# Spreading the second layer's weight conversion, summing its rows on VectorE, and adding the last two halves in the output transposes

## The chip, the core and the metric

One NeuronCore of a Trainium2 chip runs the whole program. The metric is device microseconds (us) of one execution. A profile shows one such execution, engine by engine: PE (TensorE matmuls), PEld (its weight loads), DVE (VectorE), ACT (ScalarE), POOL (GpSimd), SP (SyncE, which issues nearly all DMAs).

## What is computed

```python
# x: (2, 4096, 192), weight: (8, 7); softmax over the 7 taps
x_pad = concatenate([zeros((B, 6, D)), x], axis=1)
out = einsum('hk,bskhg->bshg', softmax(weight), windows_of_7(x_pad))   # depthwise causal convolution
x = out.reshape(8192, 192)

h = x @ w_in1                                   # (8192, 2048)
g = where(h >= 1, h, where(h <= -1, 0, (h + 1) ** 2 / 4))
x = g @ w_out1                                  # (8192, 192)

h = x @ w_in2
g = s * maximum(h, 0) ** 2 + b
return g @ w_out2                               # (8192, 192)
```

All inputs and the output are float32. Because `b` is one number, its part of the result is `b` times the sum of `w_out2` over its 2048 rows: one row of 192 biases that is added to every token.

## The kernel before

Tokens are cut into 16 blocks of 512 and `d_ff` into 16 tiles `f` of 128. A unit is one block and one tile of one layer: the first product (192 deep, giving 128 hidden rows by 512 tokens in one PSUM bank of pool `h`), the nonlinearity on ACT and DVE, and the second product, accumulated over the 16 tiles in two banks of pool `a` (128 and 64 of the 192 columns). Two blocks run side by side, so a **step** `k` is one pair of units, numbered `u = 2k` and `2k + 1`; TensorE takes them as two 64-row halves at once. There are 257 steps. Layers alternate in the order 6, 4, 4, 6, 6, 6 blocks (layer 1, layer 2, layer 1, ...), so layer 2 starts at step 48 (`u = 96`), and its tile `f` is first used at `u = 96 + 2f`.

Every operand is split into a high and a low fp32r part. For a unit of layer 1 ACT computes L1077 and L1084, DVE takes a maximum (L1090), ACT or DVE casts the high part (L385 or L387) and DVE subtracts for the low part (L1112). In layer 2 it is L1098, L1105, the cast and L1112. So each step has two L1112, and counting them tells how far DVE has come.

The weights arrive as raw words and are converted in **pieces** of two tiles (`piece`, L512): three loads on SP into one of two `raw` buffers (L523, L532, L538), then on ACT L562 and two casts, and on DVE nine instructions (L569, L577, L591, L598, L624, twice L635, L645, L654). Eight pieces hold layer 2. Line 1322 on gives piece `i` its due unit:

```python
    u0, u1 = SECOND
    for i, _ in enumerate(PIECES[1]):
        need = u0 + (u1 - u0) * (i + 1) / len(PIECES[1])
```

A block that is not convolved on TensorE is loaded by SP (L689), turned by DVE (L699) and convolved on DVE with one L715 and six L726. The 64 remaining channels of a pair of blocks are spread to both halves of the partitions by two copies SBUF to SBUF on SP's queue (L775) before they are split (L385 or L387, then L791).

The order on every engine is made ahead of time by a planner (`Plan.run`, L122). It gives each operation a priority, mostly its unit plus an offset, and a planned duration, and lets each engine take the best operation that can start. A DMA is planned at 500 ns of SP's time and 2100 ns until it has landed (L389). Engines then run their lists in order; a wait holds up all that stands behind it on the engine.

`emit_bias` (L1157) is called when the first block of layer 2 ends (after step 63). It sums `w_out2` with 16 matmuls against a matrix of ones (L1163), copies and adds the pieces of the sum (L1174, L1183), turns it (L1192) and multiplies it by `b` (L1201). The evacuation of every layer 2 block (`evac_second`, L1212) adds that bias: ACT scales 128 columns (L1225) and one half of the other 64 (L1243), then DVE adds the second half (L1252). The last two blocks leave by `put_rows` (L1293): TensorE turns 128 tokens at a time (L1300, L1301), ACT copies them out of PSUM (L385) and SP issues one DMA for each 128 tokens (L1314).

Of the kernel before, what the change touches and what calls it, by code (L numbers as in the profile page):

```python
# [28 lines left out]
SLOT, DRAIN = 232.0, 400.0  # L29


PIECES = ((1, 1) + (2,) * 7, (2,) * 8)
# [178 lines left out]
def kernel(  # L211
# [12 lines left out]
    nc = tc.nc  # L224
    B, S, D = x.shape
# [4 lines left out]
    NF = DFF // P  # L230
    NT = B * S
    NBLK = NT // NB
# [6 lines left out]
    UP, DN = slice(0, DB), slice(DB, 2 * DB)  # L239
# [6 lines left out]
    pl = Plan()  # L246

    def fixed(name, shape, dt=F32):
        return Buf(ap=const.tile(shape, dt, name=name))
# [31 lines left out]
    ident = fixed("ident", [P, P])  # L281
    ones = fixed("ones", [P, P], F32R)
# [4 lines left out]
    sb2 = fixed("sb2", [P, 2])  # L287
    bias = fixed("bias", [P, 2])
    taps = fixed("taps", [H, KT])
    band = fixed("band", [P, HG * SUB])  # L290
    toep = fixed("toep", [P, H * WIN])
    stat = fixed("stat", [H, 2])
    wsm = {"A": fixed("tapsA", [P, KT]), "B": fixed("tapsB", [P, KT])}

    def heads(_):
# [27 lines left out]
        for e in range(HG):  # L323
# [16 lines left out]
        reads=(half,),  # L340
        writes=(warm,),
# [20 lines left out]
        reads=(ident,),  # L362
        writes=(ones,),
# [546 lines left out]
    def units(k):  # L910
# [206 lines left out]
    def w_out_of(l, f):  # L1117

        i, o = at[l, f]
        return wF[l, i].ap[:, o, :]  # L1120
# [35 lines left out]

    def emit_bias(u):  # L1157

        p, row, col = Buf("h"), Buf("f"), Buf("f")
# [7 lines left out]
        ws = [wF[1, i] for i in range(len(PIECES[1]))]  # L1167
        pl.op(u + 2.6, ("pe", SLOT * NF + DRAIN), sums, reads=(ones, *ws), writes=(p,))

        for c0, c1, o in ((P, D, D), (0, P, ROW - 2 * P)):  # L1170
            pl.op(
                u + 2.7,
                act_ps(D),
                lambda _, c0=c0, c1=c1, o=o: nc.scalar.copy(  # L1174
                    row.ap[:, c0:c1], p.ap[:, o : o + c1 - c0]
                ),
                reads=(p,),
                parts=(row,),
            )
        pl.op(  # L1180
            u + 2.8,
            dve1(D),
            lambda _: nc.vector.tensor_tensor(  # L1183
                row.ap[:, 0:D], row.ap[:, 0:D], p.ap[:, 0:D], op=ALU.add
            ),
            reads=(p,),
            writes=(row,),
        )
        pl.op(
            u + 2.8,  # L1190
            dve1(D),
            lambda _: nc.vector.transpose(out=col.ap[:, 0:D], in_=row.ap[:, 0:D]),  # L1192
            reads=(row,),
            writes=(col,),
        )
        for b in range(0, D + DB, HALO):
            q, c = slice(b % P, b % P + HALO), b if b < D else b - DB
            pl.op(
                u + 2.9,
                ("dve", 120.0),  # L1200
                lambda _, b=b, q=q, c=c: nc.vector.tensor_scalar(  # L1201
                    bias.ap[q, b // P : b // P + 1],
                    col.ap[q, c : c + 1],
                    sb2.ap[q, 1:2],
                    None,
                    op0=ALU.mult,
                ),
                reads=(col, sb2),
                parts=(bias,),
            )  # L1210

    def evac_second(u, j):  # L1212

        pA, pB = acc.pop((1, j))
        q = j % 2
        me, ot = (UP, DN)[:: 1 - 2 * q]
        yA = Buf("f")
        if q == 0:
            stored["y"] = Buf("f")
        yB = stored["y"]  # L1220

        def scale(e):
            to = yA.ap[:, 0:NB]
            if e == "act":
                nc.scalar.activation(  # L1225
                    to, pA.ap, AF.Identity, bias=bias.ap[:, 0:1], scale=sb2.ap[:, 0:1]
                )
            else:
                nc.vector.tensor_scalar(
                    to, pA.ap, sb2.ap[:, 0:1], bias.ap[:, 0:1], op0=ALU.mult, op1=ALU.add  # L1230
                )

        pl.op(
            u + 3,
            (act_ps(NB, 186.0), dve1(NB, 122.0)),
            scale,
            reads=(pA, bias, sb2),
            writes=(yA,),
        )
        got = pl.op(  # L1240
            u + 3,
            act_ps(NB, 186.0),
            lambda _: nc.scalar.activation(  # L1243
                yB.ap[me, 0:NB], pB.ap[ot], AF.Identity, bias=bias.ap[me, 1:2], scale=sb2.ap[me, 0:1]
            ),
            reads=(pB, bias, sb2),
            parts=(yB,),
        )
        got = pl.op(
            u + 3.2,  # L1250
            dve1(NB, 61.0),
            lambda _: nc.vector.scalar_tensor_tensor(  # L1252
                out=yB.ap[me, 0:NB],
                in0=pB.ap[me],
                scalar=sb2.ap[me, 0:1],
                in1=yB.ap[me, 0:NB],
                op0=ALU.mult,
                op1=ALU.add,
            ),
            reads=(pB, sb2),  # L1260
            parts=(yB,),
            after=(got,),
        )
        if j >= NBLK - 2:
            put_rows(u, j, me, yA, yB, got)
            return
        put_blocks(u, yA, ((j, 0, 0, P),))
        if q:
            put_blocks(u, yB, ((j - 1, 0, P, DB), (j, DB, P, DB)))
# [20 lines left out]
                    reads=(t,),  # L1290
                )

    def put_rows(u, j, me, yA, yB, got):  # L1293

        for t in range(TT):
            p, y = Buf("h"), Buf("f")
            c = slice(t * P, (t + 1) * P)
# [5 lines left out]
            pl.op(  # L1303
                u + 5, ("pe", 500.0), turn, reads=(yA, ident), writes=(p,), parts=(yB,), after=(got,)
            )
            pl.op(
                u + 5,
                (act_ps(D), dve1(D)),
                lambda e, p=p, y=y: copy(e, y.ap[:, 0:D], p.ap[:, 0:D]),
                reads=(p,),  # L1310
                writes=(y,),
            )
            to = out[j * NB + t * P : j * NB + (t + 1) * P, :]
            dma(u + 6, lambda _, to=to, y=y: nc.sync.dma_start(out=to, in_=y.ap[:, 0:D]), reads=(y,))  # L1314


    todo = {}
# [3 lines left out]

    u0, u1 = SECOND
    for i, _ in enumerate(PIECES[1]):
# [10 lines left out]
    for i, v in enumerate((s_in, b_in)):  # L1334
        dma(
            2,
            lambda _, i=i, v=v: nc.sync.dma_start(
                out=sb2.ap[:, i : i + 1], in_=v.to_broadcast([P, 1])
            ),
            parts=(sb2,),  # L1340
            after=third,
        )

    for k in range(steps):
        for q in range(2):
            n = k + GATE - LAG * q
            if 0 <= n < len(rows[q]):
                l, j, f = rows[q][n]
# [5 lines left out]
        for q in range(2):  # L1354
# [3 lines left out]
            if l == 0 and f == 0 and j + 2 < NBLK:  # L1358
# [59 lines left out]
```

## Time and profile before

| what | us |
|---|---|
| three runs | 1200.47, 1202.11 (median), 1202.85 |
| the profiled execution | 1200.08 |
| its span, first to last instruction | 1198.1 |
| TensorE busy in the span | 1179.8 (98%) |
| VectorE busy | 808.5 (67%) |
| ScalarE busy | 863.6 (72%) |
| granted TensorE clock, mean share of full speed | 0.993 |

The profiled execution has 2.0 us outside its span, and it is 2.0 us shorter than the median run. The busy share of TensorE counts an overlap of two matmuls once, so it does not tell whether they follow each other at their best pace; the distance between the same place of two steps tells that.

### The profile page before, as it was taken

To read this page: it belongs to the slowest core of one execution; us is meant where nothing else is said; L and a number is where in the kernel's file an instruction comes from. 1 tells how busy PE (TensorE), PEld (TensorE's weight loads), DVE (VectorE), ACT (ScalarE), POOL (GpSimd) and SP (SyncE) were. 2 spreads that over 40 slices of the span, in tenths; PEclk is the share of its full clock that TensorE was granted. 3 is DMA by queue.
4 is the path that set the end of the run, shared out by engine and by line. 5 is a ranking of instruction groups with operands and counts; after the bars stand their busy time and mean duration, and the time that the engine had idled before them with its cause. 6 is when DMAs were issued, how large, how long until landed. Compare 5 with 4: busy or idle time off the path is not lost.

```text
span 1198.1 us, 24944 instructions
## 1 busy us (share of the span) xinstructions
PE 1179.8 (98%) x9900; PEld 1059.2 (88%) x9900; DVE 808.5 (67%) x1373; ACT 863.6 (72%) x1571; POOL 53.8 (4%) x528
## 2 busy tenths in 40 slices
PE   8899999999999999999999999999999999999998
PEld 7778887888889999898889888899899889999997
DVE  5997999995555696975444455787966754455543
ACT  5876878776666777787666676777777776676765
POOL 1000000000000000000000000000000000000000
PEclk8999999999999999999999999999999999999999
DMA  5431033200021111000002021111000000020100
GB/s 139 97 72 52 1 82 71 72 1 19 1 36 25 23 36 30 1 19 1 19 8 38 2 45 29 27 29 20 7 13 10 10 1 19 1 45 1 28 1 27
DMA packets 104171, 34.76 MB, mean 29 GB/s; under 512 B 86653, under 2 KB 100471, under 8 KB 104055
## 3 DMA queue, kind: packets, MB, share of 16 engines
q1 hardware_dynamic: 103703, 32.94, 13.1%
q8 instruction: 77, 1.26, 0.5%
q14 instruction: 39, 0.32, 0.1%
q10 hardware_dynamic: 352, 0.25, 0.1%
HBM read 19.53 MB, written 6.29 MB: 22 GB/s over the span
## 4 chain that ended last, share of the span: by engine, by line
PE 88%; DVE 7%; ACT 2%; DMA 1%; issue 1%; POOL 0%; SPq 0%; DVEq 0%; POOLq 0%; ACTq 0%
PE a L1019 46%; PE h L957 41%; DVE o L1112 1%; DVE f L1090 1%; DVE w L577 1%; DMA f<-x 1%; DMA x<-x 1%; DVE z L598 0%; DVE w L635 0%; PE h L894 0%; ACT f L1077 0%; ACT o L385 0%; DVE w L624 0%; PE h L472 0%; DVE z L591 0%
## 5 line engine op out<-in xcount | busy, mean ns | idle before, releaser
L1019 PE MATMUL a<-o,w 64*128 64x512 f32 (+1 forms) x5080 | 695.1, 393 | 2.6 <-ACT o L385 1.3
L1019 PEld LDWEIGHTS a<-o,w 64*128 64x128 f32 (+1 forms) x5080 | 544.7, 185 | 63.6 <-POOL seen L947 3.9
L957 PE MATMUL h<-o,w 64*128 64x512 f32 x3048 | 457.1, 392 | 2.4 <-POOL seen L947 2.4
L957 PEld LDWEIGHTS h<-o,w 64*128 64x128 f32 x3048 | 329.9, 185 | 35.6 <-POOL seen L947 6.3
L1112 DVE TENSOR_TENSOR o<-f,o 128x512 fp32r<-128x512 f32 x346 | 233.7, 687 | 15.3 <-ACT o L385 9.4
L957 PE MATMUL h<-o,wB 64*128 64x512 f32 x1536 | 234.0, 393 | 5.1 <-DVE f L1090 3.9
L385 ACT CAST o<-f 128x512 fp32r<-128x512 f32 x274 | 167.1, 621 | 42.8 <-DVE f L1090 36.4
L957 PEld LDWEIGHTS h<-o,wB 64*128 64x128 f32 x1536 | 166.1, 185 | 25.2 <-DVE f L1090 6.3
L1098 ACT ACTIVATE f<-h 128x512 f32<-128x512 f32 x167 | 95.0, 595 | 109.6 <-PE h L957 109.2
L387 DVE CAST o<-f 128x512 fp32r<-128x512 f32 x105 | 44.6, 426 | 166.2 <-ACT f L1105 166.0
L1090 DVE TENSOR_TENSOR f<-f,h 128x512 f32<-128x512 f32 x179 | 118.5, 681 | 43.9 <-ACT f L1084 43.5
L1077 ACT ACTIVATE f<-h 128x512 f32<-128x512 f32 x179 | 101.6, 595 | 47.0 <-PE h L957 46.1
L1112 DVE TENSOR_TENSOR o<-x,o 128x512 fp32r<-128x512 f32 x166 | 113.4, 687 | 6.0 <-ACT o L385 3.0
L1084 ACT ACTIVATE f<-f 128x512 f32<-128x512 f32 x179 | 108.5, 633 | 0.5
L1105 ACT ACTIVATE f<-f 128x512 f32<-128x512 f32 x167 | 101.0, 633 | 0.2
L947 POOL MEMSET seen<- 1x1 f32 x506 | 48.8, 96 | 1126.0 <-PE a L1019 566.2
L1098 ACT ACTIVATE x<-h 128x512 f32<-128x512 f32 x89 | 52.2, 595 | 63.5 <-PE h L957 63.4
L385 ACT CAST o<-x 128x512 fp32r<-128x512 f32 x132 | 81.1, 621 | 13.6 <-DVE x L1090 12.1
L387 DVE CAST o<-x 128x512 fp32r<-128x512 f32 x57 | 24.2, 425 | 96.6 <-ACT x L1105 94.7
L1090 DVE TENSOR_TENSOR x<-x,h 128x512 f32<-128x512 f32 x77 | 51.5, 681 | 29.6 <-ACT x L1084 29.4
L1077 ACT ACTIVATE x<-h 128x512 f32<-128x512 f32 x77 | 44.5, 594 | 24.2 <-PE h L957 24.2
L1105 ACT ACTIVATE x<-x 128x512 f32<-128x512 f32 x89 | 55.5, 633 | 0.1
(119 smaller groups left out, 489.6 us busy)
## 6 DMA issues: line engine op xcount, KB each, us to landing
raw<-in_moe_w_out_dram SPq DMA_DIRECT2D x15, 384.0 KB
f<-in_x_dram SPq DMA_DIRECT2D x58, 68.0 KB
raw<-in_moe_w_in_dram SPq DMA_DIRECT2D x15, 256.0 KB
out_dram<-f SPq DMA_DIRECT2D x44, 64.0 KB
out_dram<-x SPq DMA_DIRECT2D x40, 64.0 KB
f<-f SPq DMA_DIRECT2D x20, 128.0 KB
raw<-in_moe_w_in_dram SPq DMA_DIRECT2D x18, 128.0 KB
x<-f SPq DMA_DIRECT2D x16, 128.0 KB
```

Source lines behind the costliest of these rows:

```text
L385: nc.scalar.copy(to, v)
L387: nc.vector.tensor_copy(to, v)
L577: lambda _: nc.vector.scalar_tensor_tensor(out=w(True), in0=words(1), scalar=0x80000000, in1=z(True), op0=ALU.bitwise_and, op1=ALU.bitwise_or,
L947: i = nc.gpsimd.memset(seen.ap, 0.0)
L957: i = nc.tensor.matmul(h.ap, w[r], m.ap[r], start=start and n == 0, stop=stop and n == len(terms[0]) - 1,)
L1019: i = nc.tensor.matmul(p.ap, w()[r], m.ap[r], start=first and start and at_n == 0, stop=last and stop and at_n == 2,)
L1077: lambda _: nc.scalar.activation(R(), h.ap, IDENTITY_SAT15_5, scale=15.5),
L1084: lambda _: nc.scalar.activation(R(), R(), AF.Square, bias=0.5, scale=1.0 / 31.0),
L1090: lambda _: nc.vector.tensor_tensor(R(), R(), h.ap, op=ALU.max),
L1098: lambda _: nc.scalar.activation(R(), h.ap, AF.Relu),
L1105: lambda _: nc.scalar.activation(R(), R(), AF.Square),
L1112: lambda _: nc.vector.tensor_tensor(gl.ap, R(), gh.ap.bitcast(F32), op=ALU.subtract),
```

## The change

1. `SECOND` goes from `(56, 94)` to `(64, 124)`: the due unit of piece `i` of layer 2 was `60.75 + 4.75 i` (the last one at 94) and is now `71.5 + 7.5 i` (the last one at 124, the first use of its tiles).
2. `emit_bias` no longer sums `w_out2` on TensorE. As pieces become ready, 15 additions of 128x512 on DVE add up the tiles, two short ones fold the parts, and one float32 matmul of 192 columns against the ones sums over the partitions. One ACT copy takes the place of two copies and an addition.
3. For the last two blocks, the 64-column bank is scaled as a whole (128 partitions, both halves) by ACT, and a float32 matmul with `twice` (the identity's two halves added, 128x64) adds the two halves while it turns them. DVE's L1252 is gone there. Two groups of 128 tokens share an output tile, so four DMAs of twice the size replace eight.

```diff
-SECOND = (56, 94)
+SECOND = (64, 124)
...
+    twice, bias1 = toep.ap[:, 0 : D - P], toep.ap[:, D - P : D - P + 1]
...
     def emit_bias(u):
...
-        def sums(_):
-            for f in range(NF):
-                nc.tensor.matmul(
-                    p.ap, ones.ap, w_out_of(1, f)[:, P:ROW], start=(f == 0), stop=(f == NF - 1)
-                )
...
+        for f in range(1, NF):
+            pl.op(
+                u - 2 * NF + 2 * f + 4,
+                dve1(N),
+                lambda _, f=f: nc.vector.tensor_tensor(
+                    T(0, N), F(0) if f == 1 else T(0, N), F(f), op=ALU.add
...
+        for c0, c1, o in ((P, D, D), (0, P, N - P)):
...
+                    T(c0, c1), T(c0, c1), T(o, o + c1 - c0), op=ALU.add
...
+            lambda _: nc.tensor.matmul(p.ap[:, 0:D], ones.ap.bitcast(F32), T(0, D)),
...
+            lambda _: nc.scalar.copy(row.ap[:, 0:D], p.ap[:, 0:D]),
...
     def evac_second(u, j):
...
+        if j >= NBLK - 2:
+            yB = Buf("f")
+            pl.op(
+                u + 2.9,
+                ways,
+                lambda e: scale(e, yB, pB, bias1),
+                reads=(pB, toep, sb2),
+                writes=(yB,),
+            )
+            put_rows(u, j, yA, yB)
+            return
...
-                nc.tensor.transpose(p.ap[:, P:D], yB.ap[me, c], ident.ap[me, me])
...
+                nc.tensor.matmul(p.ap[:, P:D], yB.ap[:, c], twice)
...
+                        out=to, in_=y.ap[:, 0 : 2 * D].rearrange("p (t d) -> p t d", t=2)
```

In the lists below a row is a source line, an operation, the tile it writes and those it reads; lines of the changed kernel are its own (a few more than before).

SP's list where layer 2's first pieces are loaded (`moe2`), before the change; `f7<-x2` and `f0<-x2` are the SBUF copies of the first convolved pair, and `raw0`, `raw1` are the two load buffers:

```order
L523 DMA raw1_64<-in_moe2_w_in_dram 128x2x256
L532 DMA raw1_64<-in_moe2_w_in_dram 128x1x256
L538 DMA raw1_64<-in_moe2_w_out_dram 128x2x384
L775 DMA f7_74<-x2_106 64x512 x2
L775 DMA f0_67<-x2_106 64x512 x2
L523 DMA raw0_63<-in_moe2_w_in_dram 128x2x256
```

And the same place in the changed kernel, where the rows ahead of it are the load of the first piece alone:

```order
L540 DMA raw1_64<-in_moe2_w_out_dram 128x2x384
L777 DMA f7_74<-x2_106 64x512 x2
L777 DMA f3_70<-x2_106 64x512 x2
L525 DMA raw0_63<-in_moe2_w_in_dram 128x2x256
L534 DMA raw0_63<-in_moe2_w_in_dram 128x1x256
```

Three pieces stood ahead of those copies, the third one directly; now one does, and the second piece's load stands behind them. In the same way the next copies (from `x1`) stood directly behind the eighth piece's load; they now stand behind the fifth one's.

DVE's list in step 44 before the change, with a whole piece (`w1_7`) between the additions of two steps:

```order
L577 SCALAR_TENSOR_TENSOR w0_66<-raw0_63,z0_65 128x768
L791 TENSOR_TENSOR o14_92<-x0_104,o16_94 128x512
L591 TENSOR_SCALAR z0_65<-w0_66 128x768
L759 TENSOR_TENSOR o21_99<-f8_75,o17_95 128x512
L598 SCALAR_TENSOR_TENSOR z0_65<-raw0_63,z0_65 128x768
L1090 TENSOR_TENSOR f10_77<-f10_77,h3_110 128x512
L624 TENSOR_TENSOR w0_66<-w0_66,w1_7_152 128x640
L1090 TENSOR_TENSOR x2_106<-x2_106,h0_107 128x512
L635 TENSOR_TENSOR w1_7_152<-w0_66,z0_65 128x2x256
L635 TENSOR_TENSOR w1_7_152<-w0_66,z0_65 128x2x64
L1112 TENSOR_TENSOR o6_84<-f10_77,o7_85 128x512
```

The same steps of the changed kernel (`x0` holds the running sum of L1172, and `w1_5` is the sixth piece):

```order
L593 TENSOR_SCALAR z0_65<-w0_66 128x768
L1092 TENSOR_TENSOR x2_106<-x2_106,h3_110 128x512
L1092 TENSOR_TENSOR f8_75<-f8_75,h0_107 128x512
L600 SCALAR_TENSOR_TENSOR z0_65<-raw0_63,z0_65 128x768
L1114 TENSOR_TENSOR o5_83<-x2_106,o24_102 128x512
L1114 TENSOR_TENSOR o14_92<-f8_75,o18_96 128x512
L626 TENSOR_TENSOR w0_66<-w0_66,w1_5_150 128x640
L1172 TENSOR_TENSOR x0_104<-x0_104,w1_4_149 128x512
L1092 TENSOR_TENSOR x2_106<-x2_106,h2_109 128x512
L1092 TENSOR_TENSOR f4_71<-f4_71,h1_108 128x512
L637 TENSOR_TENSOR w1_5_150<-w0_66,z0_65 128x2x256
L1114 TENSOR_TENSOR o22_100<-x2_106,o1_79 128x512
```

The eighth piece was done by step 45; now the sixth is under way there, and the eighth is done in step 53. The additions of the bias sum stand between.

PE's list where the bias is summed, before the change (`a` are accumulators of layer 2, `h_107` the bank of the sum):

```order
L1019 MATMUL a_114<-o_103,w_7_152 128x512
L1019 MATMUL a_112<-o_79,w_7_152 128x512
L1163 MATMUL h_107<-w_0_145,ones 128x512 x2
...
L1163 MATMUL h_107<-w_7_152,ones 128x512 x2
L1019 MATMUL a_112<-o_93,w_7_152 128x512
```

And in the changed kernel:

```order
L1021 MATMUL a_113<-o_98,w_7_152 128x512
L1021 MATMUL a_112<-o_86,w_7_152 128x512
L1191 MATMUL h_107<-x_104,ones 128x192
L1021 MATMUL a_112<-o_90,w_7_152 128x512
L1021 MATMUL a_113<-o_96,w_7_152 128x512
```

Sixteen matmuls of 512 columns became one of 192, at the same place.

## Rows read from the trace of the kernel before

**Rows 1.** The page: engines' busy time, and the chain that ended last, by engine.
```profile
PE 1179.8 (98%) x9900; PEld 1059.2 (88%) x9900; DVE 808.5 (67%) x1373; ACT 863.6 (72%) x1571; POOL 53.8 (4%) x528
...
PE 88%; DVE 7%; ACT 2%; DMA 1%; issue 1%; POOL 0%; SPq 0%; DVEq 0%; POOLq 0%; ACTq 0%
```

**Rows 2.** The chain in order of time (start, length, what), two like places of steps.
```profile
1131.03 1.40 PE h L957 x12
...
1175.15 1.40 PE h L957 x12
```

**Rows 3.** L1112 alone in one stretch: length, busy (count), PEclk, DMA share, GB/s.
```profile
118.85:300.55 181.70, 52.10 (x79) 0.99 0.17 41
```

**Rows 4.** The same stretch in four: PE, PEld, DVE, ACT, POOL busy, PEclk, DMA, GB/s.
```profile
118.85:160.00 41.15, 40.12 (x344) 32.67 (x340) 38.79 (x63) 32.16 (x61) 1.60 (x18) 1.00 0.13 33
160.00:230.00 70.00, 69.00 (x571) 59.49 (x573) 69.18 (x125) 59.20 (x110) 2.99 (x30) 1.00 0.30 68
230.00:280.00 50.00, 47.50 (x384) 38.90 (x383) 46.75 (x80) 36.55 (x68) 3.11 (x20) 0.97 0.06 14
280.00:300.55 20.55, 20.55 (x182) 18.53 (x180) 8.43 (x15) 13.73 (x25) 0.88 (x10) 1.00 0.11 26
```

**Rows 5.** PE's waits from 110 to 300 us: total, times, longest.
```profile
PE h L957 <- DVE f L1090: 1.7, 1, 1.7
PE a L1019 <- ACT o L385: 1.3, 1, 1.3
```

**Rows 6.** The chain around the two longest stalls.
```profile
152.17 7.02 DMA f<-x
...
227.16 6.84 DMA x<-x
```

**Rows 7.** SP's timeline: a pair of SBUF copies with no load ahead.
```profile
291.73 1.10 SPq L775 DMA_DIRECT2D x<-x  x2
```

**Rows 8.** The stretch in which that pair moved (columns as in rows 4).
```profile
292.80:294.30 1.50, 1.50 (x16) 1.43 (x15) 0.00 (x0) 1.03 (x3) 0.00 (x0) 1.00 0.80 186
```

**Rows 9.** DVE's timeline in full stretches: start, length, line, operation, tiles, shapes.
```profile
137.87 0.74 DVE L726 SCALAR_TENSOR_TENSOR x<-f,tapsA,x 128x512 f32<-128x512 f32 x1
138.53 1.27 DVE L1090 TENSOR_TENSOR f<-f,h 128x512 f32<-128x512 f32 x2
...
195.69 0.95 DVE L577 SCALAR_TENSOR_TENSOR w<-raw,z 128x768 uint32<-128x768 uint32 x1
196.56 0.68 DVE L1112 TENSOR_TENSOR o<-x,o 128x512 fp32r<-128x512 f32 x1
197.16 0.68 DVE L1090 TENSOR_TENSOR f<-f,h 128x512 f32<-128x512 f32 x1
197.76 0.55 DVE L591 TENSOR_SCALAR z<-w 128x768 uint32<-128x768 uint32 x1
198.23 0.73 DVE L699 STREAM_TRANSPOSE f<-f 128x544 f32<-128x544 f32 x1
```

**Rows 10.** The chain at the bias sum.
```profile
334.00 3.92 PE h L1163 x16
```

**Rows 11.** The timeline behind it; in brackets idle time before, and its releaser.
```profile
340.13 0.78 ACT L1225 ACTIVATE f<-a,bias,sb 128x512 f32<-128x512 f32 x1 [1.79 <-DVE bias L1201]
...
341.74 0.74 DVE L1252 SCALAR_TENSOR_TENSOR f<-a,sb,f 64x512 f32<-64x512 f32 x1
342.59 0.63 PE L1019 MATMUL a<-o,w 64*128 64x512 f32 x4
```

**Rows 12.** The chain at float32 matmuls of the convolution, 120 columns each.
```profile
81.19 1.89 PE h L846 x16
```

**Rows 13.** The timeline of the end: the last copy, the output DMAs.
```profile
1192.10 2.26 SPq L1314 DMA_DIRECT2D out_dram<-f  x5
...
1194.34 0.32 ACT L385 COPY f<-h 128x192 f32<-128x192 f32 x1 [0.23 <-PE h L1301]
...
1195.41 0.39 SPq L1314 DMA_DIRECT2D out_dram<-f  x1
```

More of the change, by code (lines that the diff above doesn't have):

```diff
@@ L1157, in emit_bias @@
     def emit_bias(u):
-        p, row, col = Buf("h"), Buf("f"), Buf("f")
-        def sums(_):
-            for f in range(NF):
-                nc.tensor.matmul(
-                    p.ap, ones.ap, w_out_of(1, f)[:, P:ROW], start=(f == 0), stop=(f == NF - 1)
-                )
-        ws = [wF[1, i] for i in range(len(PIECES[1]))]
-        pl.op(u + 2.6, ("pe", SLOT * NF + DRAIN), sums, reads=(ones, *ws), writes=(p,))
-        for c0, c1, o in ((P, D, D), (0, P, ROW - 2 * P)):
+        p, col, tot = Buf("h"), Buf("f"), Buf("f")
+        row = Buf("f")
+        F = lambda f: w_out_of(1, f)[:, P:ROW].bitcast(F32)
+        T = lambda c0, c1: tot.ap[:, c0:c1]
+        N = ROW - P
+        for f in range(1, NF):
             pl.op(
[L1172 to L1175, printed above, removed]
-                ),
-                reads=(p,),
-                parts=(row,),
+                u - 2 * NF + 2 * f + 4,
+                dve1(N),
+                lambda _, f=f: nc.vector.tensor_tensor(
+                    T(0, N), F(0) if f == 1 else T(0, N), F(f), op=ALU.add
+                ),
+                reads=(wF[1, at[1, 0][0]], wF[1, at[1, f][0]]),
+                writes=(tot,),
+            )
+        for c0, c1, o in ((P, D, D), (0, P, N - P)):
+            pl.op(
+                u + 2.4,
+                dve1(c1 - c0),
+                lambda _, c0=c0, c1=c1, o=o: nc.vector.tensor_tensor(
+                    T(c0, c1), T(c0, c1), T(o, o + c1 - c0), op=ALU.add
+                ),
+                writes=(tot,),
             )
         pl.op(
[L1181 to L1185, printed above, removed]
+            u + 2.6,
+            ("pe", 400.0 + DRAIN),
+            lambda _: nc.tensor.matmul(p.ap[:, 0:D], ones.ap.bitcast(F32), T(0, D)),
+            reads=(ones, tot),
+            writes=(p,),
+        )
+        pl.op(
+            u + 2.7,
+            act_ps(D),
+            lambda _: nc.scalar.copy(row.ap[:, 0:D], p.ap[:, 0:D]),
             reads=(p,),
@@ L1210, in emit_bias @@
             )
+        pl.op(
+            u + 2.9,
+            ("dve", 130.0),
+            lambda _: nc.vector.tensor_tensor(
+                twice, ident.ap[:, UP], ident.ap[:, DN], op=ALU.add
+            ),
+            reads=(ident,),
+            writes=(toep,),
+        )
+        pl.op(
+            u + 2.9,
+            ("dve", 60.0),
+            lambda _: nc.vector.memset(bias1, 0.0),
+            writes=(toep,),
+        )
+        pl.op(
+            u + 3,
+            ("dve", 80.0),
+            lambda _: nc.vector.tensor_copy(bias1[UP], bias.ap[UP, 1:2]),
+            reads=(bias,),
+            writes=(toep,),
+        )
     def evac_second(u, j):
@@ L1217, in evac_second, with scale @@
         yA = Buf("f")
-        if q == 0:
+        if q == 0 and j < NBLK - 2:
             stored["y"] = Buf("f")
         yB = stored["y"]
-        def scale(e):
-            to = yA.ap[:, 0:NB]
+        def scale(e, to, p, b):
+            to = to.ap[:, 0:NB]
             if e == "act":
-                nc.scalar.activation(
-                    to, pA.ap, AF.Identity, bias=bias.ap[:, 0:1], scale=sb2.ap[:, 0:1]
-                )
-            else:
-                nc.vector.tensor_scalar(
-                    to, pA.ap, sb2.ap[:, 0:1], bias.ap[:, 0:1], op0=ALU.mult, op1=ALU.add
-                )
+                nc.scalar.activation(to, p.ap, AF.Identity, bias=b, scale=sb2.ap[:, 0:1])
+            else:
+                nc.vector.tensor_scalar(to, p.ap, sb2.ap[:, 0:1], b, op0=ALU.mult, op1=ALU.add)
+        ways = act_ps(NB, 186.0), dve1(NB, 122.0)
         pl.op(
             u + 3,
-            (act_ps(NB, 186.0), dve1(NB, 122.0)),
-            scale,
+            ways,
+            lambda e: scale(e, yA, pA, bias.ap[:, 0:1]),
             reads=(pA, bias, sb2),
@@ L1239, in evac_second @@
         )
+        if j >= NBLK - 2:
+            yB = Buf("f")
+            pl.op(
+                u + 2.9,
+                ways,
+                lambda e: scale(e, yB, pB, bias1),
+                reads=(pB, toep, sb2),
+                writes=(yB,),
+            )
+            put_rows(u, j, yA, yB)
+            return
         got = pl.op(
@@ L1248, in evac_second @@
         )
-        got = pl.op(
+        pl.op(
             u + 3.2,
@@ L1291, in put_blocks, with put_rows @@
                 )
-    def put_rows(u, j, me, yA, yB, got):
+    def put_rows(u, j, yA, yB):
         for t in range(TT):
-            p, y = Buf("h"), Buf("f")
-            c = slice(t * P, (t + 1) * P)
+            p, c = Buf("h"), slice(t * P, (t + 1) * P)
+            if t % 2 == 0:
+                y = Buf("f")
             def turn(_, p=p, c=c):
                 nc.tensor.transpose(p.ap[:, 0:P], yA.ap[:, c], ident.ap)
-                nc.tensor.transpose(p.ap[:, P:D], yB.ap[me, c], ident.ap[me, me])
-            pl.op(
-                u + 5, ("pe", 500.0), turn, reads=(yA, ident), writes=(p,), parts=(yB,), after=(got,)
-            )
+                nc.tensor.matmul(p.ap[:, P:D], yB.ap[:, c], twice)
+            pl.op(u + 5, ("pe", 500.0), turn, reads=(yA, yB, ident, toep), writes=(p,))
             pl.op(
@@ L1308, in put_rows @@
                 (act_ps(D), dve1(D)),
-                lambda e, p=p, y=y: copy(e, y.ap[:, 0:D], p.ap[:, 0:D]),
+                lambda e, p=p, y=y, o=t % 2 * D: copy(e, y.ap[:, o : o + D], p.ap[:, 0:D]),
                 reads=(p,),
-                writes=(y,),
+                parts=(y,),
             )
-            to = out[j * NB + t * P : j * NB + (t + 1) * P, :]
-            dma(u + 6, lambda _, to=to, y=y: nc.sync.dma_start(out=to, in_=y.ap[:, 0:D]), reads=(y,))
+            if t % 2:
+                to = out[j * NB + (t - 1) * P : j * NB + (t + 1) * P, :]
+                to = to.rearrange("(t p) d -> p t d", p=P)
+                dma(
+                    u + 6,
+                    lambda _, to=to, y=y: nc.sync.dma_start(
+                        out=to, in_=y.ap[:, 0 : 2 * D].rearrange("p (t d) -> p t d", t=2)
+                    ),
+                    reads=(y,),
+                )
     todo = {}
```

3 lines of the change are left out of this document (removed).

## The prediction

> **What bounds the kernel now.** I read the page first: TensorE is busy 98% of the span and holds 88% of the chain that ended last [rows 1]. So only what shortens or un-stalls TensorE's list counts. Busy time does not show its pace, so I took the chain late in the run, where nothing stalls: like places of two steps ten apart lie 44.12 us from each other [rows 2], 4.41 us a step. Against this pace I held the stretch in which layer 2's weights are converted. It runs from the 34th L1112 (the end of step 17) to the 112th (step 56): 181.70 us for 78 L1112 [rows 3] (the 79 counted there include one that crosses its start). At 4.41 us those 39 steps take 172.0 us. **The stretch loses 9.7 us**, the largest loss after the start-up, which the change leaves alone.
>
> Why it loses time is seen when it is cut: DVE is busy 38.79 of 41.15, 69.18 of 70.00 and 46.75 of 50.00 us, then only 8.43 of 20.55 [rows 4]. DVE is full up to about 280 us and half idle right after it. The waits of TensorE there are few, 1.7 us for L1090 and 1.3 us for a cast [rows 5], and each comes with a long transfer on the chain: SBUF copies that took 7.02 and 6.84 us [rows 6]. Both were issued right behind a piece's load in SP's list. A pair of copies with nothing ahead of it is issued from 291.73 and has moved all its bytes by 294.3, 2.6 us later [rows 7, 8]. The loss is thus of two kinds: DVE has too much to do in too few steps, and two copies come 4.5 us late. After the second one the TensorE clock drops to 1.2 GHz for a while, which the mean of 0.97 in that part shows [rows 4].
>
> The Trainium skill's page "DMA: Bandwidth & Descriptors", section "Queues, rings and completion order", says that on each DMA engine descriptors are consumed in ring order. By that rule a copy behind a load on SP's queue waits for the load's descriptors. Here 7.02 us behind a load against 2.6 us alone agrees, and so it speaks for copies that are put ahead of loads.
>
> **Part 1: pieces due later.** Its price is DVE's work per step. Instructions of DVE that follow each other without a gap start sooner than the lengths suggest: 0.60 us from one 512-column addition to the next, 0.87 for L577, 0.47 for L591, 0.66 for L726 [rows 9]. Read in this way, the nine instructions of a piece come to 4.6 us. In the order, the 39 steps held 281 DVE instructions: 152 of the 0.60 us kind (78 L1112, 61 L1090, 13 others), 36 L726, 8 pieces, 15 casts at 0.34, 6 turns and first taps at about 0.53: 160.4 us. The sum of busy time over the stretch, 163.2 us [rows 4], confirms it. The changed order holds the same pieces and taps, 6 casts fewer on DVE, and the 15 additions and two short ones of the bias sum: 167.7 us.
>
> That is more work in the same steps, yet still below their 172.0 us. What counts is where it lies. I kept a running sum along each order: DVE's work of a step less 4.41 us, never below zero. Before, it climbs from step 36 on and stands at 4.3 us in step 43 and 6.3 in step 45, where a whole piece lies between the additions of two steps; DVE cannot work that off until step 52. In the changed order it is never above 1.8 us (step 37), and is zero again within two or three steps. In steps 16 to 35 of before the same sum reaches 1.3 without lasting loss beside the first late copy; so I take 1.8 as nearly harmless.
>
> The copies: the first pair now has one piece ahead of it, whose load came long before, and the second piece's load behind it. The second pair stands behind the fifth piece, whose buffer is free seven steps earlier. Both should land in about 2.6 us. What is late next: the sixth piece's load stands behind the second pair of copies, which must wait for a tile (`x2`) that is read in step 40. Its ACT conversion is two steps (8.8 us) further on in ACT's list. A load before needs about 7 us with its issue, so with 1.2 us for the copies it may hold ACT for up to 1.5 us, and behind it the casts of one step. I take 1.5 us of remaining loss (bounds 0 and 5.5: small backlogs everywhere and one late load cost as much as the two late copies do now). **Part 1 gives 9.7 - 1.5 = 8.2 us.**
>
> First use is safe: the last piece is ready on DVE in step 53, and its tiles are first used in step 62.
>
> **Part 2: the bias sum.** The 16 matmuls take 3.92 us of the chain [rows 10] in a stretch where TensorE has no gap, so all of it returns. The new matmul is float32; the order shows one instruction where the trace of before shows two for each such matmul. In the convolution 16 such passes of 120 columns took 1.89 us [rows 12], 0.12 each; two of 192 columns make 0.38. Gross gain 3.5 us.
>
> But the 3.9 us also hid ACT and DVE. Before, the accumulator's evacuation was far ahead: L1252 frees its bank at 342.48, and TensorE writes the new block's first bank at 342.59 [rows 11] and this one 0.7 us later. Now TensorE arrives 3.5 us sooner. The chain behind it (copy, turn, eight L1201 at 0.21 us, two scalings of 0.78, a turn of 0.71 and L1252 of 0.74 [rows 11]) starts only some 1.5 us sooner, because ACT must first finish L1105, a cast and a subtraction of DVE now stand ahead in their lists, and one more DVE copy is queued. Worked through in those lengths the bank is free 6.4 us after the place of the sum begins, and TensorE wants it at 5.75: a wait of about 0.7 us. **Part 2 gives 2.8 us**, between 1.5 and 3.6.
>
> The 15 additions themselves (9.0 us at 0.60) lie under TensorE if DVE has the room that part 1 makes. If it has not, they cost up to 7.3 us, the difference of the two sums; this is the third rival.
>
> **Part 3: the end.** ACT's four scalings are as before in number and length; the L1252 that goes was parallel to them. TensorE turns at the same rate: a 64-column turn took 0.20 us in its place, two float32 passes at the 0.12 us of [rows 12] take as much (bounds: 0 to +0.1 us more for each of 8). The last copy ends at 1194.66, but SP issues its last DMA at 1195.41, because eight issues at 0.47 us each queue from 1192.10 on [rows 13]. With four, the last issue follows the last copy: 0.7 us sooner, less some 0.3 us for twice the bytes in it. **Part 3 gives 0.4 us** (-0.4 to 0.9).
>
> From step 60 to the end DVE's work by its order is the same in both programs instruction for instruction (494.7 us each), so I expect no other gain or loss there.
>
> **The sum** is 8.2 + 2.8 + 0.4 = 11.4 us, against the profiled execution's 1200.08: 1188.7. The median of the runs is 2.0 us above that execution, so for a median I predict **1190.7**.
>
> **Rivals.** (a) The late transfers only move: new collisions of copies and loads, or ACT behind the sixth load, cost what the two copies cost now (4.6 us of idle DVE), and only the overload is cured. Gain 9.7 - 5.5 + 2.3 + 0.3 = 6.8: 1195.3. For it: transfers take 7 us where 2.1 are planned; against it: the new order of SP.
>
> (b) It doesn't do what it says: DVE's overload was never what cost time, the start of the stretch and the copies were, and the bias wait takes most of part 2. Then it stays within some 2 us: 1201. Against it: DVE's idle time returns exactly where the backlog ends.
>
> (c) Slower: DVE is full, so work put on it lengthens the stretch. This decides if instructions cost their full length, about 0.08 us more than their distance. 292 instructions then make 167.7 + 23.4 = 191 us, 9.4 over the 181.7 measured; less parts 2 and 3 this gives 1202.1 + 9.4 - 3.2 = 1208.3. The skill's page "VectorE: DVE Perf Modes", section "The DRAIN you can't avoid", states such a rule: the next operation does not start until the pipeline is empty. The trace disagrees: L1112 is 0.68 us long and the next starts after 0.60 [rows 9]. By full lengths before would need 160.4 + 22.5 = 182.9 us, which, with DVE idle for 18.5 of the 181.7 [rows 4], does not fit.
>
> **How the numbers follow.** A measurement here can tell about 0.2%, 2.4 us, from no change. My forecast has a chance of 0.72, (a) 0.17, (b) 0.05, (c) 0.06. The terms' best bounds (9.7 + 3.6 + 0.9) give 1187.9 and a run's scatter a little less; (a) reaches to 1196 or so. Range 1187 to 1197. Faster comes from the forecast and (a): 0.89; same 0.05; slower 0.06.
>
> **What would show it.** Right: from step 17 to 56 some 173 to 174 us instead of 181.7, DVE busy at 95% and more until step 54 and no wait of TensorE over 1 us there; SBUF copies of some 2.6 us at the two places; no drop of the clock near 240 us. L1191 as two passes of under 0.2 us each, then a wait of TensorE below 1 us for the evacuation. The last output DMA issued within 0.2 us of the last copy. Wrong: ACT waiting for a load at the sixth piece for over 2 us, DVE waiting for a copy, a stretch that is still over 178 us long, or a wait of over 2 us behind the bias sum.

## The result, and the profile of the changed kernel

The changed kernel takes 1189.88 us (median; 1188.83 to 1190.03), before 1201.29 us in the same comparison: a ratio of 0.9902, 95% interval 0.9884 to 0.9919. The forecast was 1190.7, in a range of 1187 to 1197. The sum came out almost exactly. Its terms did not: one was 2.6 us too large, the two others were too small by 0.5 and 0.8, and two that were not in it came on top. Below, "the stretch" is steps 17 to 56, in which layer 2's weights are converted, and "the pace" the 4.41 us a step of the prediction.

The page of the changed kernel, to hold beside [rows 1]:

```profile
PE 1170.9 (99%) x9894; PEld 1049.0 (88%) x9894; DVE 812.8 (68%) x1384; ACT 865.9 (73%) x1576; POOL 53.8 (5%) x528
...
PE 91%; DVE 3%; ACT 2%; DMA 2%; issue 1%; SPq 0%; POOL 0%; DVEq 0%; ACTq 0%; POOLq 0%
```

VectorE does 4.3 us more and holds less than half of its former share of the chain. Where the 11.3 us between the spans (1198.1 and 1186.8) lie is found by following one instruction, the low-part subtraction (L1112, now L1114), through both traces; each mark in the table is the start of the last one of its step:

| stretch | before | changed | gain |
|---|---|---|---|
| start of the span to the end of step 17 | 118.14 | 116.36 | 1.8 |
| steps 17 to 56, weight conversion | 181.63 | 176.05 | 5.6 |
| steps 56 to 67, bias sum | 51.92 | 48.64 | 3.3 |
| steps 67 to 256 | 837.04 | 837.58 | -0.5 |
| from there to the end of the span | 9.4 | 8.2 | 1.2 |

The same stretch as [rows 3] and, under it, in parts as in [rows 4]:

```profile
116.36:292.41 176.05, 50.87 (x78) 0.99 0.19 45
...
116.36:160.00 43.64, 43.45 (x374) 41.56 (x374) 43.48 (x73) 35.98 (x67) 2.01 (x19) 1.00 0.16 36
160.00:230.00 70.00, 70.00 (x601) 59.37 (x599) 69.42 (x122) 61.70 (x115) 3.24 (x31) 1.00 0.26 58
230.00:270.00 40.00, 38.08 (x310) 32.44 (x308) 36.12 (x63) 31.99 (x60) 1.52 (x17) 0.96 0.17 50
270.00:292.41 22.41, 22.41 (x196) 20.53 (x194) 20.56 (x38) 14.69 (x28) 1.10 (x10) 1.00 0.06 14
...
236.00:246.00 10.00, 9.78 (x69) 7.93 (x71) 10.00 (x17) 8.73 (x18) 0.27 (x3) 0.83 0.11 35
```

VectorE is now busy evenly to the end, and up to 230 us TensorE is idle for no more than 0.2 us. One part still loses: from 230 to 270 us TensorE is idle for 1.9 us, VectorE for 3.9, and the mean of the granted clock falls to 0.96, that is, a while at 1.2 GHz (the last row shows the 10 us around it). Of the 4.1 us that the stretch takes above the pace, TensorE is idle for 2.1; a mean clock of 0.83 over 10 us is a third of them at half speed, by an estimate another 1.7 us. The waits of ScalarE and TensorE in the stretch name the place (compare [rows 5]):

```profile
ACT z L564 <- DMA raw<-in_moe_w_out_dram: 3.8, 1, 3.8
...
PE a L1021 <- ACT o L387: 1.8, 1, 1.8
```

And the timeline of SyncE and ScalarE there:

```profile
224.46 1.49 SPq L777 DMA_DIRECT2D x<-x  x2
226.00 0.59 SPq L525 DMA_DIRECT2D raw<-in_moe_w_in_dram  x1
226.62 0.57 SPq L534 DMA_DIRECT2D raw<-in_moe_w_in_dram  x1
227.24 0.47 SPq L540 DMA_DIRECT2D raw<-in_moe_w_out_dram  x1
227.75 0.47 SPq L525 DMA_DIRECT2D raw<-in_moe_w_in_dram  x1
...
229.24 1.15 ACT L1086 ACTIVATE f<-f 128x512 f32<-128x512 f32 x2
234.18 0.89 ACT L564 ACTIVATE z<-raw 128x768 f32<-128x768 f32 x1 [3.79 <-DMA raw<-in_moe_w_out_dram]
234.97 1.12 ACT L387 CAST o<-f 128x512 fp32r<-128x512 f32 x2
```

It is the sixth piece. SyncE holds the copies (L777) until the tile that they overwrite has been read, and the load (L525 and the next two) stands behind them; it is used 8.2 us after its first issue (226.00 to 234.18). ScalarE reaches the conversion at 230.4 us and stands still for 3.8 us with two casts behind it, for which TensorE waits 1.8 us.

At the place of the bias sum the chain holds the first row instead of [rows 10]; the second is the scaling of the evacuation, in ScalarE's timeline:

```profile
326.75 0.52 PE h L1191 x2
...
330.14 0.78 ACT L1262 ACTIVATE f<-a,bias,sb 128x512 f32<-128x512 f32 x1 [1.67 <-DVE bias L1214]
```

TensorE waits for nothing from step 56 to 67. At the end (timeline, beside [rows 13]) four transfers leave, the last one 0.02 us behind the last copy:

```profile
1180.40 0.27 PE L1343 MATMUL h<-ident,f 128*128 128x128 f32 x1
...
1180.68 0.28 PE L1343 MATMUL h<-ident,f 128*128 128x128 f32 x1
...
1183.22 0.60 ACT L387 COPY x<-h 128x192 f32<-128x192 f32 x2
1183.84 0.37 SPq L1359 DMA_DIRECT2D out_dram<-x  x1
```

The same turns before the change, two groups that follow each other:

```profile
1190.91 0.33 PE L1300 MATMUL h<-ident,f 128*128 128x128 f32 x1
...
1191.37 0.33 PE L1300 MATMUL h<-ident,f 128*128 128x128 f32 x1
```

### The profile page after: what moved, and what is told of

Its sections match the earlier page's. It is cut to its first block, busy times and chain, and to the rows that moved or that the text cites. A ratio compares the mean times of both kernels' runs of the same rounds, so it can differ in the third digit from the quotient of the medians.

```text
span 1186.8 us, 24940 instructions
## 1 busy us (share of the span) xinstructions
PE 1170.9 (99%) x9894; PEld 1049.0 (88%) x9894; DVE 812.8 (68%) x1384; ACT 865.9 (73%) x1576; POOL 53.8 (5%) x528
## 4 chain that ended last, share of the span: by engine, by line
PE 91%; DVE 3%; ACT 2%; DMA 2%; issue 1%; SPq 0%; POOL 0%; DVEq 0%; ACTq 0%; POOLq 0%
PE a L1021 48%; PE h L959 43%; DMA raw<-in_moe_w_in_dram 1%; DVE o L1114 1%; DMA raw<-in_moe_w_out_dram 1%; DVE f L1092 1%; DVE w L579 0%; ACT f L1079 0%; DVE z L600 0%; ACT o L387 0%; DVE w L637 0%; DVE w L626 0%; ACT z L564 0%; PE h L875 0%; ACT f L1086 0%
## 5 line engine op out<-in xcount | busy, mean ns | idle before, releaser
L1114 DVE TENSOR_TENSOR o<-f,o 128x512 fp32r<-128x512 f32 x344 | 231.9, 686 | 16.5 <-ACT o L387 10.7
L387 ACT CAST o<-f 128x512 fp32r<-128x512 f32 x287 | 175.5, 621 | 38.1 <-DVE f L1092 35.4
L389 DVE CAST o<-f 128x512 fp32r<-128x512 f32 x93 | 39.5, 426 | 146.1 <-ACT f L1107 146.0
L1114 DVE TENSOR_TENSOR o<-x,o 128x512 fp32r<-128x512 f32 x168 | 114.6, 687 | 5.0 <-ACT o L387 2.1
L389 DVE CAST o<-x 128x512 fp32r<-128x512 f32 x63 | 26.8, 425 | 103.5 <-ACT x L1107 103.5
L387 ACT CAST o<-x 128x512 fp32r<-128x512 f32 x125 | 77.3, 621 | 12.0 <-DVE x L1092 10.4
```

The source lines that it names most:

```text
L1114: lambda _: nc.vector.tensor_tensor(gl.ap, R(), gh.ap.bitcast(F32), op=ALU.subtract),
```

## Experiments

The theory behind them: the stretch of the conversions lost time before in two ways (VectorE's running backlog, and copies that came late behind loads), and what it still loses is the late sixth load alone. The rivals: VectorE is full and loses whatever else is mended; or only transfers matter and the backlog is harmless. Each run's time is a median, its ratio is to the kernel before on the same chip (1200.7 to 1201.3 us there).

**The parts alone.** First the due units:

```diff
-SECOND = (56, 94)
+SECOND = (64, 124)
```

> The kernel before with nothing but the due units of the second layer's pieces changed, (64, 124). The changed kernel ran steps 17 to 56 in 176.05 us where before took 181.6. Theory A (part 1 is that gain, and what it still loses is ScalarE waiting 3.8 us for the sixth piece's load, which stands behind copies in SyncE's list here too): 176 us again in that stretch, with a wait of ScalarE for a load of 3 us or more, no change behind it, in all 1201.3 - 5.6 = 1195.7 us. Theory B (the additions of the bias sum fill VectorE in the changed kernel and cost part of the gain): 173 to 174 us in the stretch, in all about 1193.5.

Measured: 1190.38 us, 0.9907 (0.9891 to 0.9922). The stretch by all engines (columns as in [rows 4], here and below), and the sixth load in SyncE's timeline:

```profile
118.15:290.04 171.89, 171.68 (x1473) 153.84 (x1473) 162.91 (x282) 142.13 (x262) 8.41 (x77) 1.00 0.20 48
...
227.50 0.59 SPq L523 DMA_DIRECT2D raw<-in_moe_w_in_dram  x1
```

Both expectations missed. 171.9 us is the pace itself: with the due units alone nothing is lost there, the whole 9.7 us come back, and ScalarE waits for no load, though SyncE issues the sixth load as late here (227.5 us). ScalarE's list tells why: here the conversion of that piece comes after 45.5 steps of ScalarE's own work, in the changed kernel after 43.5. So the late load of the changed kernel comes in with the bias sum.

Second, the bias sum alone in the kernel before (additions L1172 and L1183, the one matmul, its copy):

```diff
-                    p.ap, ones.ap, w_out_of(1, f)[:, P:ROW], start=(f == 0), stop=(f == NF - 1)
...
+                    T(0, N), F(0) if f == 1 else T(0, N), F(f), op=ALU.add
...
+            lambda _: nc.tensor.matmul(p.ap[:, 0:D], ones.ap.bitcast(F32), T(0, D)),
```

> The kernel before with nothing but the bias sum moved to VectorE. Its order puts 169.6 us of VectorE work into steps 17 to 56 (160.4 before), with a running backlog of 4 to 6 us from step 41 to step 53. Theory A (VectorE's backlog costs time in this stretch): the 3.3 us that the place of the sum gave back, less 1 to 4 us of a longer stretch (183 to 185 us instead of 181.6): 1199 to 1201. Theory B (only late transfers cost time there, backlog does not): the stretch stays at 181.6, in all 1201.3 - 3.3 = 1198.0.

Measured: 1199.18 us, 0.9985 (0.9977 to 0.9994). The stretch, and TensorE's waits for VectorE in it:

```profile
118.43:301.72 183.29, 177.95 (x1473) 153.44 (x1473) 171.58 (x299) 141.68 (x261) 7.75 (x77) 0.99 0.17 39
...
PE h L957 <- DVE x L1090: 2.0, 2, 1.0
PE h L957 <- DVE f L1090: 1.3, 2, 1.1
```

Theory A: the sum's place gives 3.3 us (51.92 to 48.63), the stretch takes 1.0 to 1.7 back (three profiles with the stretch of the kernel before took 181.6 to 182.3). So the additions are not free there, where VectorE has a backlog already; the late copies of before are in this run too (6.2 and 7.1 us on its chain).

Third, the end alone, that is the last two blocks' path:

```diff
-                nc.tensor.transpose(p.ap[:, P:D], yB.ap[me, c], ident.ap[me, me])
+                nc.tensor.matmul(p.ap[:, P:D], yB.ap[:, c], twice)
...
+                        out=to, in_=y.ap[:, 0 : 2 * D].rearrange("p (t d) -> p t d", t=2)
```

> The kernel before with nothing but the last two blocks' halves added in the turns and four output transfers instead of eight. In the changed kernel the last VectorE operation to the end of the run shortened by about 1.1 us. Theory A (fewer output transfers at the end, as predicted, 0.4 us, or up to 1.1): 1200.2 to 1200.9, first 1170 us as before. Theory B (the end is no shorter, the 1.1 us came from elsewhere): 1201.3.

Measured: 1199.33 us, 0.9984 (0.9976 to 0.9993); from the last subtraction to the end 8.0 us instead of 9.4, the rest as before. Theory A, with 1.4 us at the place where 0.4 to 1.1 were expected.

**The late load.** One piece may be issued four units earlier; every other engine's list stays:

```diff
-        todo.setdefault(max(int(need) - AHEAD, 0), []).append((1, i, need))
+        todo.setdefault(max(int(need) - (AHEAD if i != 5 else 26), 0), []).append((1, i, need))
```

> The changed kernel with one thing moved: the load of the sixth piece stands ahead of the copies from x1 in SyncE's list (it may be issued four units earlier); the orders of TensorE, ScalarE, VectorE and GpSimd are the same row for row. Theory A (what the stretch still loses, 4.0 us, is that load coming late): no wait of ScalarE for a load at the sixth piece, no TensorE wait over 1 us there, no drop of the clock near 240 us, steps 17 to 56 in 172.5 to 173.5 us instead of 176.05: 1189.9 - 3 = 1187 us. Theory B (VectorE is 97 per cent busy there, so what the load no longer costs is lost to VectorE's own work): about 175.5 us, in all 1189.4.

Measured: 1186.7 us, 0.9876 (0.9862 to 0.9889). The stretch, then the load in SyncE's timeline and the conversion in ScalarE's:

```profile
118.13:290.24 172.11, 171.84 (x1473) 147.46 (x1473) 169.22 (x293) 144.18 (x267) 7.74 (x77) 1.00 0.20 46
...
206.32 0.37 SPq L525 DMA_DIRECT2D raw<-in_moe_w_in_dram  x1
...
230.92 1.15 ACT L1086 ACTIVATE f<-f 128x512 f32<-128x512 f32 x2
231.96 0.89 ACT L564 ACTIVATE z<-raw 128x768 f32<-128x768 f32 x1
```

The load goes 20 us earlier, the conversion follows without a gap, and the stretch is back at 172.1 us while VectorE does the same work. The rival that VectorE's fullness is what remains falls: at 98% busy (169.22 of 172.11) it costs 0.1 us.

**Copies or backlog?** In the kernel before, dependencies put both pairs of copies ahead of the loads that they stood behind (`loads` holds the loads of a piece):

```diff
+        loads[l, i] = (first, got)
...
+            held = {(0, 4): (2, 3), (0, 5): (2, 3), (1, 0): (7,), (1, 1): (7,)}.get((l, j), ())
+            hold = [o for i in held for o in loads[1, i]]
             for r in (UP, DN):
-                dma(
+                last = dma(
...
+                for o in hold:
+                    o.deps.add(last)
+                    last.users.append(o)
+                    o.missing += 1
```

> The kernel before with only SyncE's list changed: both pairs of copies SBUF to SBUF stand ahead of the load that they stood behind (third and eighth piece); the orders of the other engines are the same row for row, so VectorE's running backlog is still 6.3 us at its highest. Steps 17 to 56 took 181.6 us there, 171.9 with the later due units alone. Theory A (the two late copies cost 4.6 us and the backlog the rest): about 177 us, in all 1201.0 - 4.6 = 1196.4. Theory B (only late transfers cost time, the backlog is harmless): 172 to 173 us, in all about 1192. Theory C (only the backlog does): 181 us, no gain.

Measured: 1194.86 us, 0.9945 (0.9932 to 0.9957). The stretch, and the chain where the second late copy stood (6.84 us in [rows 6]):

```profile
118.75:294.69 175.94, 174.17 (x1473) 157.16 (x1473) 162.66 (x282) 141.80 (x261) 7.96 (x77) 1.00 0.18 42
...
226.93 0.60 DVE o L1120
227.53 0.60 DVE o L761
228.13 0.60 DVE o L1120
...
230.70 0.95 DVE w L578
231.65 0.60 DVE f L1098
...
233.06 0.87 DVE z L599
233.92 0.73 DVE w L625
234.66 0.60 DVE o L1120
235.26 0.80 DVE w L636 x2
```

Theory A in mechanism and nearly in size: the copies cost 5.7 us (4.6 expected) and are gone from the chain; in their place stands VectorE, a piece's instructions between the additions, and the 4.0 us that are still lost against the pace are put down to it. The profile of the kernel before was one of its faster executions (1200.08 us): by the medians of this set the copies cost 6.5 us. Moving them ahead of loads in one queue's list, with no other list changed, took their 7 us off the chain. This agrees with the rule of the Trainium skill's page "DMA: Bandwidth & Descriptors", section "Queues, rings and completion order", that descriptors are consumed in ring order. Whether a copy behind a load waits for its turn or shares the DMA engines with the load, the run does not part.

**What the bias sum is worth beside the others.** The changed kernel with the sum left on TensorE:

```diff
-                    T(0, N), F(0) if f == 1 else T(0, N), F(f), op=ALU.add
...
+                    p.ap, ones.ap, w_out_of(1, f)[:, P:ROW], start=(f == 0), stop=(f == NF - 1)
```

> The changed kernel with the bias sum left on TensorE (16 matmuls), that is the due units and the end of the change alone. Theory A (in the changed kernel the moved bias sum gives 3.3 us at its place and takes 4 us, because with it ScalarE's list has the sixth piece's conversion two steps earlier, ahead of its load): steps 17 to 56 in 172 us, the bias place 3.3 us longer, the end 0.9 us shorter than before: 1190.4 - 0.9 = 1189.5, no more than 0.5 us from the changed kernel. Theory B (the late load is there in any case): 176 us in the stretch and 1193.

Measured: 1188.29 us, 0.989 (0.9876 to 0.9904). The stretch and steps 56 to 67:

```profile
116.96:288.79 171.83, 171.62 (x1473) 157.89 (x1472) 162.86 (x281) 142.13 (x262) 8.44 (x77) 1.00 0.20 48
288.79:340.77 51.98, 51.98 (x430) 44.80 (x428) 28.38 (x56) 34.42 (x64) 1.85 (x21) 1.00 0.07 12
```

Theory A in the stretch: no late load, no loss; the total is 1.2 us below what it gave, and step 17 ends 1.2 us sooner than in the first run (116.96 and 118.15 us). As built, the second part of the change gains 3.3 us at its place and loses 4.2 in the stretch. With the -0.5 us of the later steps that is a small loss, and without this part the median is 1.6 us below the changed kernel's 1189.88 and 0.5 below the 1188.78 that it has further down. These were measured on different chips, and the intervals of their ratios overlap: in total, part 2 as built is not shown to gain or to lose.

**How much room VectorE has.** Each addition of L1172 twice, with the early load:

```diff
         for f in range(1, NF):
+            for _ in range(2):
...
```

> The changed kernel with the early sixth load and each of the 15 additions of the bias sum done twice (the row sum comes out nearly doubled). 9.0 us more work for VectorE by the distance of 0.60 us; its order then has 171.7 us in steps 17 to 56 and a running backlog of 3.5 us at most. Theory A (an addition costs its distance, and a backlog under 4 us costs little): 172.5 to 174 us in the stretch, 1187 to 1189 in all. Theory B (VectorE is already full at 97 per cent busy, each addition lengthens the run): about 181 us, in all 1195.7.

And all pieces of layer 2 released earlier, the sixth among them:

```diff
-        todo.setdefault(max(int(need) - AHEAD, 0), []).append((1, i, need))
+        todo.setdefault(max(int(need) - 30, 0), []).append((1, i, need))
```

> The changed kernel with every piece of the second layer released eight units earlier (30 instead of 22 units ahead of its due unit). The sixth load again stands ahead of the copies, but VectorE's order changes: its running backlog reaches 4.2 us in step 43 and stays between 2 and 4 us from step 36 to step 54. Theory A (a backlog of this size costs some time): 173 to 175 us in steps 17 to 56 (172.1 with the one load moved), in all 1187.5 to 1189.5. Theory B (the backlog is harmless as long as transfers come in time): 172.1 us, 1186.7.

Measured: 1187.29 us, 0.9879 (0.9862 to 0.9895), and 1187.56 us, 0.9884 (0.9871 to 0.9898). The stretch in the first, the stretch and a wait of ScalarE in the second:

```profile
118.56:292.01 173.45, 172.72 (x1476) 152.40 (x1476) 172.72 (x303) 143.16 (x265) 8.73 (x77) 1.00 0.18 44
```

```profile
118.81:292.13 173.32, 172.56 (x1473) 154.63 (x1473) 169.77 (x295) 143.36 (x265) 8.40 (x77) 1.00 0.18 41
...
ACT z L564 <- DMA f<-in_x_dram: 1.0, 1, 1.0
```

Theory A in both: 9 us of extra additions, by which these steps hold 4.0 us more of VectorE's work by the order, cost 1.3 us of the stretch, and the higher backlog 1.2 (some of that can be the wait of 1.0 us, which the run does not part from it). The extra additions also moved ScalarE's last four conversions one or two steps back (the sixth to 45.5 again), so 1.3 us is the price of that whole order.

**A second profile of three kernels.** The kernel before, the changed kernel and the one with the early load again, on one chip:

> The kernel before once more, unchanged, for a second profile of it. In the first pair of profiles the changed kernel reached the end of step 17 at 116.4 us and before at 118.1, though the change moves nothing there. Theory A (scatter of the start, of the first transfers): step 17 ends anywhere from 116.4 to 118.8, as in the other profiles; steps 17 to 56 near 181.6 us, and its runs spread over 4 us as before. Theory B (the start of before is always at 118 and the changed kernel gains there): 118.1 again, and 116.4 in the other run of this pair.

> The changed kernel once more, unchanged, for a second profile and beside the one with the early sixth load. Theory A: the wait of ScalarE for the sixth piece's load is there again with 3 to 4 us and steps 17 to 56 take 175.5 to 176.5 us, the end of step 17 lies between 116.4 and 118.8; 1189 to 1190.5 in all. Theory B (that wait was an accident of one execution): 172 to 173 us in the stretch.

> The changed kernel with the sixth load ahead of the copies, again, on the same chip as the changed kernel itself. Theory A: 172 us in steps 17 to 56, 3 us below the changed kernel, 1186.5 to 1187. Theory B (the first measurement's chip was faster): within 1 us of the changed kernel.

Measured: 1201.22, 1188.78 and 1186.87 us. The load's wait is no accident (3.7 us again, 175.59 us in the stretch), and with the early load the stretch takes 172.17 us. That version is the fastest of all, 1.9 us below the changed kernel here, where 3 were expected: its stretch is 3.4 us shorter, but its step 17 ends 2.3 us later. So the first theory A on the start, scatter, did not hold where it could be tested: step 17 ends at 118.60 us in before and at 116.24 in the changed kernel again. TensorE's list is the same through the first thousand instructions, but from 9 to 20 us the granted clock (third number from the end, a mean of stretches at 1.2 and at 2.4 GHz) differs. Before, before again, changed, changed again:

```profile
9.00:20.00 11.00, 10.75 (x81) 10.61 (x82) 6.24 (x18) 5.34 (x13) 0.00 (x0) 0.69 0.45 120
```

```profile
9.00:20.00 11.00, 10.08 (x76) 9.98 (x77) 6.50 (x19) 4.95 (x12) 0.00 (x0) 0.69 0.44 119
```

```profile
9.00:20.00 11.00, 10.65 (x89) 9.73 (x88) 7.58 (x20) 5.93 (x14) 0.00 (x0) 0.84 0.48 129
```

```profile
9.00:20.00 11.00, 10.81 (x91) 9.85 (x90) 7.58 (x20) 6.02 (x14) 0.00 (x0) 0.84 0.51 137
```

In these 11 us the changed kernel gets through 89 or 91 matmuls where before does 81 or 76. The kernel with the sum on TensorE has 0.84 there too and ended step 17 at 116.96; all others have 0.53 to 0.69 and ended it at 118.1 to 118.8. What in a program sets this was not found.

## Why the prediction was right, and where it was not

**Part 1, the reading: right.** The loss of 9.7 us against the pace was real, all of it: the due units alone brought the stretch to 171.9 us. Its two causes were there as told, and the runs size them: late copies 5.7 us in the profiles (6.5 by the medians), and 4.0 left for the backlog (the prediction had them together, and 4.6 for the copies in rival (a)). The running sum made from the orders goes with what a backlog costs: at a highest value of 1.8 to 2.0 us nothing (171.8 to 172.2), at 3.5 about 1.4, at 4.2 at most 1.3, at 6.3 about 4.0. Its height is not all: with the bias sum alone it is 4 to 6 us and no higher than before, but from step 41 to step 53, and the stretch is longer.

**Part 1, the size: too large by 2.6 us.** The step that failed is "it may hold ACT for up to 1.5 us". The place and the mechanism were right, both lengths in it were not: from the issue of the copies to ScalarE's arrival at the conversion it is 5.9 us, not 8.8, since ScalarE did the work of these two steps without a halt instead of at TensorE's pace; and copies and load together took 9.7 us, not 8.2. The difference is the 3.8 us of wait. By the prediction's own lengths (7 and 1.2 us against 8.8) the load would have been in time by 0.6 us, so its 1.5 us did not come out of them; it was an allowance. The prediction took 1.5 us of remaining loss and gave 5.5 as the other end; it was 4.1, against the 172.0 us of the pace. It put this on the due units, and there it was wrong too: the first run, and the one with the sum left on TensorE, show that it needs the bias sum, which changes where the planner puts the sixth conversion. The sign of being wrong that it named, ScalarE waiting for over 2 us at the sixth piece, thus came (3.8 us), and three signs of being right did not: the stretch took 176 us instead of 173 to 174, TensorE waited for over 1 us in it, and the clock fell near 240 us.

**Part 2: 3.3 us at its place, 2.8 forecast.** The wait of 0.7 us for the evacuation did not come: ScalarE starts the scaling at 330.14 us, 3.4 us after the matmul begins, and TensorE never waits from 292 to 341 us. The matmul took 0.52 us instead of 0.38, two passes of 0.26 where under 0.2 was expected. What the part costs elsewhere was taken as nothing "if DVE has the room that part 1 makes". VectorE had it; the list of ScalarE did not, and that is the 4.2 us of the stretch.

**Part 3: 1.2 us, 0.4 forecast, 0.9 its upper bound.** That the last transfer follows the last copy was right (0.02 us instead of 0.75). The step "TensorE turns at the same rate" was not: the first groups are 0.28 us apart, where before they were 0.46, so the last copy is earlier too. The two are worth 0.7 us each; from its issue to the end of the span the last transfer takes 0.3 us longer, as the prediction had it.

**What was not in the sum**: 1.8 us at the start, in a part that the change was not meant to touch, and -0.5 us between steps 67 and 256. The latter is there in each profile that has both the later due units and the bias sum on VectorE (837.3 to 837.6 us) and in none without (837.0 to 837.2); its cause is open. So 8.2 + 2.8 + 0.4 became 5.6 + 3.3 + 1.2 - 0.5 + 1.8: the total was right partly by luck, and without the start it would be 9.6. These are the terms of two profiled executions; the changed kernel's is 1.05 us faster than the median of its runs, and how much of the 1.8 us the other runs have is not shown.

**The rivals.** (a) had the mechanism that came true, a load in place of a copy, at 4.1 us of loss in the stretch; its total (1195.3) did not come, since the other terms were larger. (b) falls with the first run, (c) with the fourth: 293 instructions lay in 172.1 us, where full lengths ask for 191. The sentence of the Trainium skill's page "VectorE: DVE Perf Modes", section "The DRAIN you can't avoid", on which (c) drew, that the next operation does not start until the pipeline is empty, would by itself have made (c) true. The same paragraph says that a next operation which is not held starts earlier; the prediction left that out, and the trace shows such starts (0.60 us from start to start of operations 0.68 us long, [rows 9]).

## What to carry to other kernels

Where an engine's list is fixed ahead, sum its work step by step against the pace of the engine that bounds the kernel: a total that fits says little, the height of the running backlog and how long it stays say more (here nothing was lost at 2 us, 4 at 6.3). Then walk each load's queue with the times of the trace: what stands ahead of it, when that can leave, and when the consumer really arrives, which can be sooner than the distance in steps says (here 5.9 us for two steps of 4.41). And measure the parts together: a gain at one place (here 3.3 us) can be paid back at another (4.2) because the same planner moves one conversion by two steps.

## What was not expected of the hardware

Late copies do not only cost time, they scatter it: on one chip nine runs of the kernel before ranged from 1199.0 to 1203.3 us, and with the copies alone put ahead of the loads five runs lay between 1194.64 and 1195.02. And a program's first 17 steps can be 1.8 to 2.4 us shorter with the same list of TensorE instructions, at a higher granted clock from 9 to 20 us (0.84 against 0.69); the three programs that were profiled twice kept to their side both times.
